# Where each engine reads the kind of the next block: at the head of the loop, or inside the arms into a register that lives across iterations

## The chip, the cores and the metric

One core of a Trainium2 chip runs the kernel. The metric is the device time of one execution in microseconds (us); the median of three executions before the change is 526.78 us (526.13 to 526.92).

## What is computed

The reference is a sigmoid attention followed by a mixture of experts in which only some tokens take part. Attention has 8 batches, 12 heads, 448 positions and a head size of 64; its output, turned to 3584 tokens of 768 numbers, is the input x of the second part:

```python
scores = scale * np.matmul(q, k.transpose(0, 1, 3, 2)) - np.log(S)
attn = 1.0 / (1.0 + np.exp(-scores))
x = (attn @ v)                       # reshaped to 3584 x 768
...
do_compute = x @ w_skip > 0          # the other tokens keep x
e_idx = argmax(x @ w_gate)           # one of 8 experts
gate_w = softmax(x @ w_gate)[e_idx]
out = x + gate_w * (relu(x @ w1[e_idx]) @ w2[e_idx])
```

Here w1 is 768 x 1024 and w2 is 1024 x 768 for each expert, in float32.

## The kernel before

The first part, up to about 321 us of the span, is straight-line code: attention, the routing of the tokens to experts, and the first blocks of tokens. Behind it stands a loop (L1537) whose trip count and whose work depend on the data; here it runs 14 times, from about 321 to 523 us. One iteration handles one block of up to 128 tokens of one expert, and there are four kinds of block, each with its own code (an "arm"):

- FULL (`block(i, False)`): a block of 128 tokens, with the weights split into a high and a low part (wh, wl) so that three products make one in float32. First product L516, turn of h L530, second product L544.
- SPLIT (`block(i, True)`): the same, and the weights of the next expert are split in its course (L1231, L1234, L1237).
- HALF (`half`): up to 64 tokens, both products at L1458, two at a time side by side in the array, turn of h at L1481.
- FEW (`few`): up to 32 tokens, both products at L1391, four at a time side by side, turn of h at L1412 (first half) and L1416 (second half).

The kinds in the order of this input are SPLIT, HALF, FULL, HALF, FULL, FEW, FULL, FEW, FULL, FEW, SPLIT, FEW, FULL, FEW.

A table `slots` of three rows (L1086) holds per block whether there is a next expert, which one, and the kind (row TYP). `entry` (L1088) reads one number of it into a register of each engine named, with an assertion on its bounds; on an engine this is a TENSOR_LOAD with a FUSED_REGOPS for the address ahead of it (both shown at L1089). At the head of the loop all five engines load the kind of block i, `slots[TYP, i + 2]`, and take two compare-and-branch instructions (`choose`, L1525 to L1533) into the arm. The five engines run through the loop each at its own pace; semaphores alone tie them together. Within an arm the order is written by hand (`tc.manual_schedule`). SP also reads in each FEW and HALF and in each SPLIT the next expert (`next_expert`) and starts the transfers of its weights (L1213, L1222).

The helpers that the steps below name: `turn_x` transposes the gathered tokens of the next block on PE (L492, into pxt); `fetch` lets POOL gather the tokens of the block after it (L564) and its records (L1115); `ready_x` and `whole_x` bring the turned tokens into the forms that the products want (ACT L498 and L1097, DVE L502); `shift` moves a list of indices on by one on DVE (L1283); `weigh_sum` multiplies the products py with the gate on DVE (L1325); `put` adds the block to the output by an indirect transfer of POOL (L574); `advance` moves the records on (L1315 to L1318).

```python
def entry(j, col, engines, most):
    return nc.values_load(slots[j : j + 1, col], engines=engines, min_val=0, max_val=most)
...
with tc.For_i(0, nreg, 1, iteration_sync="reg_based") as i:
    kind = entry(TYP, ds(i + 2, 1), mybir.ALL_ENGINES, SPLIT)
    choose(kind, i)
```

Of the kernel before, what the change touches and what calls it, by code (L numbers as in the profile page):

```python
# [23 lines left out]
def kernel(  # L24
# [11 lines left out]
    nc = tc.nc  # L36
# [471 lines left out]
    def gemm1(h, part, xh, xl, ph, lag=False):  # L508

        kinds = ((xh, wh1), (xh, wl1), (xl, wh1))  # L510
        t = [(2 * j + 3 * (n == 2) if lag else 2 * n * NK1, n, j) for n in range(3) for j in range(NK1)]
        t.sort()
        for n in part:
            _, kind, j = t[n]
            a, w = kinds[kind]
            nc.tensor.matmul(  # L516
                ph[h],
                a[:, j * P : (j + 1) * P],
                w[j][h],
                start=(n == 0),  # L520
                stop=(n == len(t) - 1),
            )

    def relu(h, hs, ph):
        nc.scalar.activation(hs[:, h * H1 : (h + 1) * H1], ph[h], AF.Relu)  # L525
# [579 lines left out]
    def ready_x():  # L1105
        for h in range(2):
            hi_x(h, pxt[h], xh)
        for h in range(2):
            whole_x(h, [slice(j, j + 1) for j in range(3)])
        for h in range(2):  # L1110
            lo_x(h, pxt[h], xh, xl)
# [128 lines left out]
        nc.vector.tensor_tensor(wl2[i], raw2[i], wh2[i], op=ALU.subtract)  # L1240

    dve, pool = nc.vector, nc.gpsimd

    order.__exit__(None, None, None)
    nx = (
# [81 lines left out]
    def block(i, last):  # L1327


        def split1(js, h):  # L1330
            if last:
                for j in js:
                    hi1(j, h)
                for j in js:
                    lo1(j, h)

        gemm1(0, range(G1), xh, xl, ph, last)
        relu(0, hs, ph)
        split1(range(3), 0)
        gemm1(1, range(9), xh, xl, ph, last)  # L1340
        turn_h(0, hs, pht[0])
        split_h(0, pht[0], hh, hl)
        take_rec()
        split1(range(3, NK1), 0)
        gemm1(1, range(9, G1), xh, xl, ph, last)
        relu(1, hs, ph)
        for h in range(2):
            turn_x(xn, h, pxt[h])
        fetch()
        split1(range(3), 1)  # L1350
        gemm2(0, hh, hl, py)
        turn_h(1, hs, pht[1])
        split_h(1, pht[1], hh, hl)
        split1(range(3, NK1), 1)
        if last:
            for h in range(2):
                whole_x(h, (slice(0, 3),))
            shift(dve)
        else:
            ready_x()  # L1360
        for j in range(1, NK2):
            gemm2(j, hh, hl, py)
        if last:
            for j in range(2):
                hi2(j)
            for h in range(2):
                hi_x(h, pxt[h], xh)
            for j in range(2, NK2):
                hi2(j)
            for j in range(4):  # L1370
                lo2(j)
            for h in range(2):
                lo_x(h, pxt[h], xh, xl)
        else:
            shift(dve)
        for o in range(2):
            rows = ys if last else yt
            weigh_sum(rows[:, o * H2 : (o + 1) * H2], half_y(py, o), recs[:, 0, 0:1])
        put(P, last)
        advance(1 if last else 2)  # L1380
        if last:
            for j in range(4, NK2):
                lo2(j)

    def few(i):

        nx = next_expert(ds(i + 2, 1))
        take_rec()

        def quarter(dst, g, n, a, w, j, most):  # L1390
            nc.tensor.matmul(  # L1391
                dst[g * SM : (g + 1) * SM, :n],
                a,
                w,
                start=(j == 0),
                stop=(j == most - 1),
                tile_position=(0, g * SM),
            )

        Q1 = FF // 4  # L1400
        turned = (pht[0], ph[0])
        parts = [slice(c * P, (c + 1) * P) for c in range(2)]
        for c, s in enumerate(parts):
            for j in range(NK1):
                for g in range(4):
                    at = (g % 2) * Q1 + c * P
                    quarter(ph[c], g, P, xf[:, j, :SM], raw1[j][g // 2][:, at : at + P], j, NK1)
            nc.scalar.activation(hs[:, s], ph[c][:, :P], AF.Relu)
        for h in range(2):
            for g in range(2):  # L1410
                load_w1(g, h, nx)
        nc.tensor.transpose(turned[0][:, :P], hs[:, parts[0]], ident)  # L1412
        for h in range(2):
            turn_x(xn, h, pxt[h])
        fetch()
        nc.tensor.transpose(turned[1][:, :P], hs[:, parts[1]], ident)  # L1416
        ht4 = ht[:, : 8 * SM].rearrange("p (c g t) -> p c g t", c=2, g=4)
        for s, p in zip(parts, turned):
            nc.scalar.activation(ht[:, s], p[:, :P], AF.Copy)
        ready_x()  # L1420
        shift(dve)

        for n, j in enumerate((0, 2, 1, 3)):
            for g in range(4):
                o, h = g // 2, g % 2
                m = j + h * (NK2 // 2)
                quarter(
                    py[h],
                    g,
                    H2,  # L1430
                    ht4[:, j % 2, 2 * h + j // 2, :],
                    raw2[m][:, o * H2 : (o + 1) * H2],
                    n,
                    NK2 // 2,
                )
        for g in range(4):
            load_w2(g, nx)
        for m in range(2):
            for o in range(2):
                g = 2 * o + m  # L1440
                s = slice(o * H2, (o + 1) * H2)
                p = py[m][g * SM : (g + 1) * SM, :H2]
                if not m:
                    nc.scalar.activation(yt[:SM, s], p, AF.Copy, scale=recs[:SM, 0, 0:1])  # L1444
                    continue
                nc.vector.scalar_tensor_tensor(
                    yt[:SM, s], p, recs[:SM, 0, 0:1], yt[:SM, s], op0=ALU.mult, op1=ALU.add
                )
        put(SM)
        advance()  # L1450

    def half(i):

        nx = next_expert(ds(i + 2, 1))
        take_rec()

        def side(dst, g, n, a, w, j, most):
            nc.tensor.matmul(  # L1458
                dst[g * MD : (g + 1) * MD, :n],
                a,  # L1460
                w,
                start=(j == 0),
                stop=(j == most - 1),
                tile_position=(0, g * MD),
            )

        for j in range(NK1):
            for h in range(2):
                side(ph[0], h, H1, xf[:, j, :], raw1[j][h], j, NK1)
        turned = (pht[0], ph[1])  # L1470
        parts = [slice(0, 2 * P), slice(2 * P, 4 * P)]
        for s in (slice(0, P), slice(P, 2 * P), parts[1]):
            nc.scalar.activation(hs[:, s], ph[0][:, s], AF.Relu)
        for h in range(2):
            for g in range(2):
                load_w1(g, h, nx)
        for h in range(2):
            turn_x(xn, h, pxt[h])
        fetch()
        for c in range(4):  # L1480
            nc.tensor.transpose(  # L1481
                turned[c // 2][:, (c % 2) * P : (c % 2 + 1) * P],
                hs[:, c * P : (c + 1) * P],
                ident,
            )
        for s, p in zip(parts, turned):
            nc.scalar.activation(ht[:, s], p[:, : 2 * P], AF.Copy)
        ready_x()
        shift(dve)

        ht8 = ht.rearrange("p (c h t) -> p c h t", c=4, h=2)
        for n in range(NK2):
            c, h = divmod(n, 2)
            m = h * (NK2 // 2) + c
            for o in range(2):
                side(
                    py[1],
                    o,
                    H2,
                    ht8[:, c, h, :],  # L1500
                    raw2[m][:, o * H2 : (o + 1) * H2],
                    n,
                    NK2,
                )
        for g in range(4):
            load_w2(g, nx)
        for o in range(2):
            s = slice(o * H2, (o + 1) * H2)
            weigh_sum(ys[:MD, s], py[1][o * MD : (o + 1) * MD, :H2], recs[:MD, 0, 0:1])
        put(MD)  # L1510
        advance()
# [13 lines left out]
    def choose(kind, i):  # L1525
# [5 lines left out]
        with c.Else():  # L1531
            with tc.If(kind < SPLIT) as d:
                run(HALF, i)  # L1533
            with d.Else():
                run(SPLIT, i)

    with tc.For_i(0, nreg, 1, iteration_sync="reg_based") as i:  # L1537
        kind = entry(TYP, ds(i + 2, 1), mybir.ALL_ENGINES, SPLIT)
        choose(kind, i)


# [26 lines left out]
```

## Time and profile before

| what | value |
|---|---|
| median of three executions | 526.78 us (526.13 to 526.92) |
| the profiled execution, its own time | 526.53 us |
| its span on the core | 524.8 us |
| granted TensorE clock, mean | 0.995 |
| instructions | 15310 |
| DMA traffic | 107.21 MB, mean 204 GB/s |

The profile is of one execution. In its rows PE is TensorE's matmuls, PEld its weight loads, DVE VectorE, ACT ScalarE, POOL GpSimd and SP SyncE; a "q" behind the engine's name is an instruction of the engine's sequencer (a register load, a branch, a semaphore), which doesn't count as busy. L12 is line 12 of the kernel. An entry "out<-in" names what an instruction writes and reads. The share of the clock and the busy shares of PE over the span, in 40 slices of 13.1 us:

```profile
PE   8999999999999999999989999999999999999991
PEclk9999999999999999999999999999999999999997
```

PE is busy in all slices but the last, and at full clock; the loop covers the last 16 of them.

### The profile page before, as it was taken

Reading aid. Unit: us, or ns where it says so; the run is one execution under the profiler, and the core shown is the slowest. Engines: PE = TensorE matmul, PEld = TensorE weight load, DVE = VectorE, ACT = ScalarE, POOL = GpSimd, SP = SyncE. Lnnn points to the kernel's source line nnn. Section 1 sums busy time; section 2 is a strip of 40 time slices with the busy share of each in tenths; the row PEclk is TensorE's granted clock in tenths of the full one; section 3 lists DMA queues with packets and bytes.
Section 4 is the critical chain, followed back from the end, with each engine's and each line's share of the span. In section 5 each row is a group of like instructions: output and inputs, shape, how many; then the busy total and the mean of one; then the engine's idle time right before and its main releaser. Section 6 shows DMA issues by size and latency. Waiting matters only on the chain.

```text
span 524.8 us, 15310 instructions
## 1 busy us (share of the span) xinstructions
PE 508.7 (97%) x5033; PEld 339.2 (65%) x5034; DVE 296.1 (56%) x721; ACT 281.0 (54%) x485; POOL 262.5 (50%) x414
## 2 busy tenths in 40 slices
PE   8999999999999999999989999999999999999991
PEld 7765555545545456555445989948669797978790
DVE  4556757648667676687684962862222322269422
ACT  5776776767767668677664211942112323268322
POOL 4523553443557666766574332553333645455644
PEclk9999999999999999999999999999999999999997
DMA  8999787898999999999955023979393959695942
GB/s 211 209 257 200 150 187 156 178 175 173 195 206 234 220 203 221 196 204 213 199 105 114 11 92 105 389 210 347 99 364 119 317 230 310 240 328 227 346 184 47
DMA packets 140288, 107.21 MB, mean 204 GB/s; under 512 B 97099, under 2 KB 112731, under 8 KB 140240
## 3 DMA queue, kind: packets, MB, share of 16 engines
q1 hardware_dynamic: 134000, 97.66, 70.0%
q0 software_dynamic: 4576, 8.65, 6.9%
q8 instruction: 30, 0.49, 0.4%
q10 hardware_dynamic: 1664, 0.26, 0.3%
q14 instruction: 18, 0.15, 0.1%
HBM read 98.49 MB, written 17.56 MB: 221 GB/s over the span
## 4 chain that ended last, share of the span: by engine, by line
PE 89%; DVE 3%; SPq 2%; DMA 2%; issue 1%; ACT 1%; POOL 0%; POOLq 0%; ACTq 0%; DVEq 0%
PE s L212 23%; PE pa L240 21%; PE ph L516 11%; PE py L544 11%; PE b_ph L516 3%; PE b_py L544 3%; PE ph L1391 3%; PE py L1458 2%; PE ph L1458 2%; PE pxt L492 2%; PE py L1391 2%; PE pl L280 1%; PE pht L530 1%; DMA out_dram<-y 1%; SPq L263 1%
## 5 line engine op out<-in xcount | busy, mean ns | idle before, releaser
L232 ACT ACTIVATE at<-s,bias 128x896 f32<-128x896 f32 (+1 forms) x191 | 173.3, 913 | 82.1 <-PE s L212 71.2
L212 PE MATMUL s<-x 64*64 64x448 f32 (+1 forms) x1528 | 165.4, 498 | 1.3 <-DVE wh L485 0.9
L240 PE MATMUL pa<-at,v 64*64 64x448 f32 (+1 forms) x1536 | 163.0, 489 | 0.0
L176 POOL COPY kq<-kq 32x896 f32<-32x896 f32 (+1 forms) x96 | 88.1, 917 | 94.6 <-DMA kq<-in_q_dram 59.0
L212 PEld LDWEIGHTS s<-x 64*64 64x64 f32 x1528 | 80.0, 191 | 53.1 <-issue 28.6
L240 PEld LDWEIGHTS pa<-at,v 64*64 64x64 f32 x1536 | 62.5, 133 | 54.9 <-issue 47.8
L194 DVE STREAM_TRANSPOSE x<-kq 128x448 f32<-128x448 f32 x94 | 80.8, 934 | 5.0 <-POOL kq L176 5.0
L250 DVE TENSOR_TENSOR xt<-xt,pa 128x448 f32<-128x448 f32 x48 | 29.7, 620 | 54.4 <-ACT xt L673 49.6
L414 POOL DMA_INDIRECT lst<-rec,idx x32 | 31.7, 989 | 17.4 <-DVE xt L250 5.8
L486 POOL TENSOR_TENSOR wl<-wr,wh 128x384 fp32r<-128x384 f32 (+1 forms) x28 | 31.2, 1125 | 12.6 <-DVE wh L485 8.1
L255 DVE STREAM_TRANSPOSE y<-xt 128x448 f32<-128x448 f32 x48 | 31.0, 645 | 6.8 <-DMA out_dram<-y 5.2
L574 POOL DMA_INDIRECT out_dram<-ys,rp x15 | 23.7, 1580 | 16.6 <-issue 8.4
L525 ACT ACTIVATE hs<-ph 128x512 f32<-128x512 f32 x14 | 8.3, 596 | 43.9 <-PE ph L516 37.5
L536 DVE TENSOR_TENSOR hl<-pht,hh 128x512 fp32r<-128x512 f32 x14 | 9.7, 690 | 36.5 <-ACT hh L535 22.8
L544 PE MATMUL py<-wh,hh 128*128 128x384 f32 x112 | 29.8, 347 | 0.0
L502 DVE TENSOR_TENSOR xl<-pxt,xh 128x384 fp32r<-128x384 f32 x30 | 15.3, 552 | 25.3 <-ACT xf L1097 17.8
L544 PE MATMUL py<-wh,hl 128*128 128x384 f32 x112 | 28.8, 338 | 0.0
L544 PE MATMUL py<-wl,hh 128*128 128x384 f32 x112 | 28.7, 337 | 0.0
L516 PE MATMUL ph<-wh,xh 128*128 128x512 f32 x84 | 25.7, 402 | 1.1 <-ACT yt L1444 0.8
L516 PE MATMUL ph<-wl,xh 128*128 128x512 f32 x84 | 26.6, 403 | 0.0
L673 ACT ACTIVATE xt<-pa 128x448 f32<-128x448 f32 x48 | 25.7, 536 | 0.8 <-PE pa L240 0.8
L516 PE MATMUL ph<-wh,xl 128*128 128x512 f32 x84 | 24.5, 395 | 0.0
(277 smaller groups left out, 686.4 us busy)
## 6 DMA issues: line engine op xcount, KB each, us to landing
raw<-in_moe_w_dram SPq DMA_DIRECT2D x64, 768.0 KB
v<-in_v_dram SPq DMA_DIRECT2D x48, 256.0 KB
out_dram<-y SPq DMA_DIRECT2D x192, 56.0 KB
kq<-in_k_dram SPq DMA_DIRECT2D x46, 224.0 KB
kq<-in_q_dram SPq DMA_DIRECT2D x46, 224.0 KB
wr<-in_moe_w_dram SPq DMA_DIRECT2D x12, 256.0 KB
wr<-in_moe_w_dram SPq DMA_DIRECT2D x16, 192.0 KB
lst<-fill SPq DMA_DIRECT2D x4, 464.0 KB
```

The source lines that it names most:

```text
L176: nc.gpsimd.tensor_copy(a[BT:, :, :, :BT], a[:BT, :, :, BT:])
L194: nc.vector.transpose(xs[:, n].rearrange("p (r j) -> p j r", j=NJ), t.rearrange("p (j d) -> p j d", d=D)[:, :, :BT],)
L212: nc.tensor.matmul(sc[m * D : (m + 1) * D, j, : qs.stop - qs.start], xs[r, 0, first::NR7], xs[r, 1, qs], start=True, stop=True,)
L232: nc.scalar.activation(at[:, :, :n], sc[:, :, :n], AF.Sigmoid, bias=bias, scale=SCALE)
L240: nc.tensor.matmul(pa[j * D : (j + 1) * D, r, qs], vt[rs, j, r + c if c < 3 else 3 * (1 - r), :], at[rs, j, : qs.stop - qs.start], start=( ...
L250: nc.vector.tensor_tensor(x, x, pa[:, 1, :S], op=ALU.add)
L255: nc.vector.transpose(y, xts[b][:, hp, :])
L414: put = nc.gpsimd.indirect_dma_start(out=lst[:, :], out_offset=bass.IndirectOffsetOnAxis(ap=idx[:, c : c + 1], axis=0), in_=rec[:, c, :], ...
L486: nc.gpsimd.tensor_tensor(lo, r, hi, op=ALU.subtract)
L516: nc.tensor.matmul(ph[h], a[:, j * P : (j + 1) * P], w[j][h], start=(n == 0), stop=(n == len(t) - 1),)
L544: last = nc.tensor.matmul(half_y(py, o), a[h][:, js], w[j][:, o * H2 : (o + 1) * H2], start=(j == 0 and n == 0), stop=(j == NK2 - 1 and n ...
L1391: nc.tensor.matmul(dst[g * SM : (g + 1) * SM, :n], a, w, start=(j == 0), stop=(j == most - 1), tile_position=(0, g * SM),)
```

## The change

Each engine gets one register, `kinds`, that holds the kind of the block to come. It is loaded once ahead of the loop, from column 2. In each arm a new call, `next_kind`, loads column i + 3 into it, for each engine at a place of its own; the head of the loop only takes the register for the two comparisons.

```diff
+    kinds = nc.alloc_registers("kind", engines=mybir.ALL_ENGINES)
+
+    def next_kind(i, *engines):
+        for e in engines:
+            nc.engines[e].reg_mov(kinds[e], entry(TYP, ds(i + 3, 1), [e], SPLIT))
...
     def block(i, last):
...
+        next_kind(i, ET.SP)
         gemm1(0, range(G1), xh, xl, ph, last)
...
         relu(1, hs, ph)
+        next_kind(i, ET.PE)
         for h in range(2):
             turn_x(xn, h, pxt[h])
         fetch()
+        next_kind(i, ET.Pool)
         split1(range(3), 1)
...
             shift(dve)
+            next_kind(i, ET.DVE)
         else:
             ready_x()
+        next_kind(i, ET.Activation)
         for j in range(1, NK2):
             gemm2(j, hh, hl, py)
...
         else:
             shift(dve)
+            next_kind(i, ET.DVE)
         for o in range(2):
...
     def few(i):
         nx = next_expert(ds(i + 2, 1))
+        next_kind(i, ET.SP)
         take_rec()
...
         fetch()
+        next_kind(i, ET.Pool)
+        next_kind(i, ET.PE)
         nc.tensor.transpose(turned[1][:, :P], hs[:, parts[1]], ident)
...
         ready_x()
         shift(dve)
+        next_kind(i, ET.Activation, ET.DVE)
...
     def half(i):
         nx = next_expert(ds(i + 2, 1))
+        next_kind(i, ET.SP)
         take_rec()
...
         fetch()
+        next_kind(i, ET.PE, ET.Pool)
         for c in range(4):
...
         ready_x()
         shift(dve)
+        next_kind(i, ET.Activation, ET.DVE)
...
+    nc.regs_mov(kinds, entry(TYP, slice(2, 3), mybir.ALL_ENGINES, SPLIT))
     with tc.For_i(0, nreg, 1, iteration_sync="reg_based") as i:
-        kind = entry(TYP, ds(i + 2, 1), mybir.ALL_ENGINES, SPLIT)
+        kind = nc.snap(kinds, min_val=0, max_val=SPLIT)
         choose(kind, i)
```

Lines of the changed kernel behind the new function stand 7 to 21 lines later than before (the loop is L1558, the second turn of h in FEW L1432).

Three places in the program's order show what moved. The first is DVE at the entry into the loop, behind the last instruction of the straight-line code (L559), with the semaphores that an instruction waits for; before:

```order
L502 TENSOR_TENSOR xl<-pxt,xh 128x384 [waits PE_49,Activation_49]
L502 TENSOR_TENSOR xl<-pxt,xh 128x384
L559 SCALAR_TENSOR_TENSOR ys<-b_py,rc_3732,x_3781 128x384 [waits DMASW5_49,PE_49]
L559 SCALAR_TENSOR_TENSOR ys<-b_py,rc_3732,x_3781 128x384
L1537 COMPARE_AND_BRANCH [waits DVE_I-4406_own,DVE_sequencer_I-4406_own]
L1537 UNCONDITIONAL_BRANCH
L1563 BRANCH_PREFETCH_HINT
L1089 ISA
L1089 TENSOR_LOAD slots [waits DVE_49]
```

and in the changed kernel:

```order
L502 TENSOR_TENSOR xl<-pxt,xh 128x384 [waits PE_49,Activation_49]
L502 TENSOR_TENSOR xl<-pxt,xh 128x384
L559 SCALAR_TENSOR_TENSOR ys<-b_py,rc_3732,x_3781 128x384 [waits DMASW5_49,PE_49]
L559 SCALAR_TENSOR_TENSOR ys<-b_py,rc_3732,x_3781 128x384
L1089 TENSOR_LOAD slots [waits DVE_49]
L1558 COMPARE_AND_BRANCH [waits DVE_I-4425_own,DVE_sequencer_I-4425_own]
L1558 UNCONDITIONAL_BRANCH
L1584 BRANCH_PREFETCH_HINT
```

The load now stands ahead of the first branch of the loop, and so ahead of the semaphores that go with it; the address computation (ISA) has gone, since the column is fixed. The other engines' entries change in the same way.

The second place is PE in FEW, from the turn of the first half of h (L1412) to the second product; before:

```order
L1391 MATMUL ph_4373<-raw_0_1_4348,xf 32x128 x2
L1391 MATMUL ph_4373<-raw_1_1_4366,xf 32x128 x2
L1412 ISA
L1412 MATMUL pht<-ident,hs 128x128
L492 REGISTER_ALU
L492 MATMUL pxt<-ident,xn 128x128 x6
L1416 REGISTER_ALU
L1416 MATMUL ph_4372<-ident,hs 128x128
L1391 ISA
L1391 MATMUL py_4374<-raw_0_4367,ht 32x384
```

and in the changed kernel, where these lines are L1426, L1432 and L1405:

```order
L1405 MATMUL ph_4373<-raw_0_1_4348,xf 32x128 x2
L1405 MATMUL ph_4373<-raw_1_1_4366,xf 32x128 x2
L1426 ISA
L1426 MATMUL pht<-ident,hs 128x128
L492 REGISTER_ALU
L492 MATMUL pxt<-ident,xn 128x128 x6
L1089 ISA
L1089 TENSOR_LOAD slots
L1089 ISA x2
L1248 ISA
L1432 MATMUL ph_4372<-ident,hs 128x128
L1405 ISA
```

Five instructions have come between the turn of x (L492) and the second turn of h: the address, the load, two for the assertion, and one at L1248 for the register.

The third place is PE in FULL and SPLIT, from the end of the first product (L516) to the second (L544); one piece of the difference, with + for what is new:

```order
 L516 MATMUL ph_4373<-wh_4_1_101,xl 128x512
 L516 MATMUL ph_4373<-wh_5_1_103,xl 128x512
+L1089 ISA
+L1089 TENSOR_LOAD slots
+L1089 ISA x2
 L492 MATMUL pxt<-ident,xn 128x128 x6
 L544 ISA
```

The load stands there ahead of the turn of x, with nothing else moved.

More of the change, by code (lines that the diff above doesn't have):

```diff
@@ L1242 @@
     dve, pool = nc.vector, nc.gpsimd
+    ET = mybir.EngineType
+    kinds = nc.alloc_registers("kind", engines=mybir.ALL_ENGINES)
+    def next_kind(i, *engines):
+        for e in engines:
+            nc.engines[e].reg_mov(kinds[e], entry(TYP, ds(i + 3, 1), [e], SPLIT))
     order.__exit__(None, None, None)
```

## Prediction

> **What bounds the kernel now.** I read the page first (busy time, then the chain that ended last), then the cost of the loads that the change moves, then the heads of the loop and the waits around them.
>
> ```profile
> span 524.8 us, 15310 instructions
> PE 508.7 (97%) x5033; PEld 339.2 (65%) x5034; DVE 296.1 (56%) x721; ACT 281.0 (54%) x485; POOL 262.5 (50%) x414
> PE 89%; DVE 3%; SPq 2%; DMA 2%; issue 1%; ACT 1%; POOL 0%; POOLq 0%; ACTq 0%; DVEq 0%
> ```
>
> TensorE is busy 97% of the span and carries 89% of the chain; nothing else is above 56%. So an edit is worth what it does to the matmul array's rare idle places, and to the tail behind the last matmul. What the change moves are sequencer instructions. The rows of their line in before (the "q" is the engine's sequencer; nanoseconds, least/median/most):
>
> ```profile
> L1089 PEldq TENSOR_LOAD <-slots x14: 302/310/1265, 321.9 to 505.0; - x14
> L1089 DVEq TENSOR_LOAD <-slots x14: 305/317/331, 324.9 to 509.7; - x14
> L1089 ACTq TENSOR_LOAD <-slots x14: 12/278/291, 321.5 to 502.6; - x14
> L1089 POOLq TENSOR_LOAD <-slots x14: 295/302/311, 326.6 to 510.8; - x14
> L1089 PEldq FUSED_REGOPS  x14: 51/51/56, 321.7 to 504.9; - x14
> L1089 SPq FUSED_REGOPS  x42: 46/152/342, 335.1 to 516.7; - x42
> L1089 SPq SEQ_ASSERT  x28: 5/18/23, 335.4 to 516.9; - x28
> ```
>
> A load takes about 0.3 us of its sequencer, but PE's longest took 1.27 us. Whether that reaches the array shows in the chain of waits across heads (start, length, what):
>
> ```profile
> 399.91 3.87 PE py L544 x22
> 403.78 2.77 PE ph L1391 x96
> ...
> 407.58 2.75 PE py L1391 x32
> 410.34 6.49 PE ph L516 x27
> ...
> 432.71 2.75 PE py L1391 x32
> 435.47 0.28 issue
> 435.75 4.43 PE ph L516 x18
> ```
>
> At 403.78 (FULL to FEW) and 410.34 (FEW to FULL) the array goes on without a break, though PE's sequencer loads and branches there: it had queued enough work. At 435.47 the array ran dry for 0.28 us. One other head shows this, in the timeline:
>
> ```profile
> 461.75 0.47 PE L516 MATMUL ph<-wh,xh 128*128 128x512 f32 x1 [0.80 <-ACT yt L1444]
> ```
>
> The releaser named there, ACT, comes from the last semaphore; PE's own loads around those two places, beside the other two heads behind a FEW, are
>
> ```profile
> L1089 PEldq TENSOR_LOAD <-slots x1: 459/459/459, 409.1 to 409.1; - x1
> L1089 PEldq TENSOR_LOAD <-slots x1: 972/972/972, 434.3 to 434.3; - x1
> L1089 PEldq TENSOR_LOAD <-slots x1: 1265/1265/1265, 459.7 to 459.7; - x1
> L1089 PEldq TENSOR_LOAD <-slots x1: 446/446/446, 487.1 to 487.1; - x1
> ```
>
> The two long ones, 434.3 + 0.97 = 435.3 and 459.7 + 1.27 = 461.0, end shortly before the array starts again. They are the only heads at which I find the load on the array's path.
>
> **The change, part by part.** *PE's head without its load.* Gain: 0.28 + 0.80 = **1.08 us** at most, 0 at the other heads. I take all of it: the long load ends last there. The low end is 0, if the stall belongs to the place and not to the load. Nothing behind these two places takes the gain back as long as the whole is not earlier than before, since the weights' transfers keep their times.
>
> *The first loads, now ahead of the loop.* On every engine the load (and a move into the register) stands now before the semaphore updates that open the loop. The timeline of the first iteration's start shows who waits for those:
>
> ```profile
> 323.55 0.40 PE L516 MATMUL ph<-wh,xh 128*128 128x512 f32 x1
> 323.75 1.14 DVE L559 SCALAR_TENSOR_TENSOR ys<-b_py,rc,x 128x384 f32<-128x384 f32 x2 [0.52 <-PE b_py L544]
> 323.84 0.19 PEld L516 LDWEIGHTS ph<-wl,xh 128*128 128x128 f32 x1 [0.27 <-DVEq L1537]
> ...
> L1537 DVEq EVENT_SEMAPHORE  x2: 21/21/21, 323.8 to 323.9; - x2
> ...
> L1537 DVEq MOVE  x1: 43/43/43, 324.7 to 324.7; - x1
> ...
> L1060 DVEq TENSOR_LOAD <-left_i x1: 556/556/556, 306.1 to 306.1; - x1
> ```
>
> The second matmul of the loop has waited 0.27 us for DVE's update, and DVE could issue that only when L559 had been let go by PE. Now a load and a move come between: 0.32 (median of L1089) + 0.04 + two gaps between instructions of about 0.07 (the end of one row to the start of the next at the head) = 0.50 us. With 0.56 us, the load from a fixed address at L1060, it would be 0.74. If DVE's sequencer were not held by L559, it would be 0. I take **+0.5 us**: the update's start, 323.8, follows L559's, 323.75, at once, so the sequencer was held. Nothing behind can absorb it, since the array is dense from there on. For PE itself the load only changes places ahead of a queue that is full (loaded at 321.9, needed at 323.55).
>
> *PE's load in FEW.* It now stands behind the turn of x (L492) and ahead of the second transpose of h (L1416). In the first FEW:
>
> ```profile
> 406.68 0.28 ACT L1408 ACTIVATE hs<-ph 128x128 f32<-128x128 f32 x1 [0.95 <-PE ph L1391]
> ...
> 407.20 0.14 PEld L1416 LDWEIGHTS ph<-ident,hs 128*128 128x128 f32 x1
> ...
> 407.51 0.20 PEld L1391 LDWEIGHTS py<-raw,ht 128*32 128x32 f32 x8 [0.17 <-issue]
> ...
> L1416 PEldq ALU_OP  x1: 32/32/32, 406.4 to 406.4; - x1
> ...
> L1416 PEldq ALU_OP  x1: 32/32/32, 484.0 to 484.0; - x1
> L1416 PEld LDWEIGHTS ph<-ident,hs x1: 137/137/137, 485.4 to 485.4; 128*128 128x128 f32 x1
> ...
> L1391 PEldq FUSED_REGOPS  x1: 37/37/37, 407.0 to 407.0; - x1
> ```
>
> The sequencer reaches L1416 at 406.4 and gets to the next instruction (L1391) only at 407.0, right after ACT's hs has ended at 406.96: it is held there for nearly 0.6 us. New work in that hold: address 0.05, load 0.31, the two steps of the bounds assertion 0.15 and 0.02 (SP's rows), the move 0.04, and five gaps of 0.07: 0.92 us. The 0.6 are free, **0.3 us** are not, and the next matmul (L1391, "issue" 0.17) is bound by the sequencer already, so they reach the array. The second and third FEW look alike; the fourth is held 1.4 - 0.8 = 0.6 us longer and hides all; the fifth is the last iteration, whose end is not set by PE. So 3 x 0.3 = **+0.9 us**. The ends: 0 where the hold or the queue covers all; and, with loads as long as 0.97 to 1.27 us, another 0.66 to 0.96 us (0.97 and 1.27 less 0.31) in each of three, 2.0 to 2.9 us in all. I take 0.31, because the array is then at transposes as wide as the matmuls under which the other ten loads stayed near it, and not at the 32-column ones under which all four slower loads fell.
>
> [...]
>
> *PE's load in FULL, SPLIT and HALF.* In the blocks it stands ahead of the turn of x, and the sequencer's next long wait is
>
> ```profile
> L544 PEldq EVENT_SEMAPHORE  x7: 960/1047/1427, 330.2 to 495.3; - x7
> ```
>
> The least of these seven waits, 0.96 us, covers the 0.92. In HALF the head's evidence holds: a load of this size costs a full queue nothing. **0**; with that cover gone it would be 0.92 us in each.
>
> *The other engines.* ACT, POOL and DVE each lose 0.3 us at the head and get about 0.9 us in the arm. POOL's stands behind the issue of its gathers and waits for DVE anyway (41.0 us below); ACT's stands in stretches where ACT waits for PE (37.5); SP trades the load at the head for one ahead of weights that stream over many microseconds.
>
> ```profile
> POOL jk L1293 <- DVE sv L1315: 41.0, 9, 5.6
> ACT hs L525 <- PE ph L516: 37.5, 8, 8.1
> DVE yt L1325 <- PE py L544: 17.7, 5, 3.6
> ```
>
> DVE's stands between the shift of the indices and the weighing of y, where in FULL it waits for PE (17.7). In FEW nothing waits on PE's side for yt; only in the last FEW is it near the end of the chain, where POOL's use of yt comes about 1 us behind it: 0 here, 0.3 at worst. **0** in all.
>
> Sum: -1.08 + 0.5 + 0.9 = **+0.3 us**. The profiled execution took 526.53 us, 1.73 more than its span, and lies 0.25 below the median of the runs, 526.78. The sum gives 526.85 from the one and 527.1 from the other; I say **526.9**.
>
> **The rivals.** *The added loads are hidden, the removed stalls are gone.* Then -1.08 alone: 525.5 on the profiled execution; with the start's 0.5 kept, 525.95. For it: 403.78 and 410.34, where the queue hid the same load. Against it: the hold at L1416 and the update at 323.8. [...]
>
> *The stalls belong to the place.* PE's 0.97 and 1.27 us would then be something else that lands on whatever stands there, and the idle 1.08 us stays: +0.5 + 0.9 = +1.4, 527.9. For it: two other loads at the same place took 0.45 only, so the length is not the load's own. Against it: none of the rows beside it is as long.
>
> *Slower: PE's load in FEW is long there, too.* The price is the 2.0 to 2.9 us above on top of +0.3: 528.8 to 529.7. It decides from a load of 0.31 us on, since everything beyond the hold goes to the array one for one. For it: all four loads above 0.4 us fell around FEW. Against it: those fell under the packed second product, this one falls behind the first.
>
> **How the numbers follow.** What a measurement of this kernel can tell from no change is about 0.2%, 1.05 us. Forecast 0.50; hidden loads 0.20; the stalls stay 0.17; long loads in FEW 0.13. Forecast, with 0.2 to 0.6 us of spread in each term, is "same" but for 0.05 on the slower side. Hidden loads lie at -0.6 to -1.1, at the bound: 0.12 faster, 0.08 same. Stalls that stay, at +1.4: 0.09 slower, 0.08 same. Long loads: slower, 0.13. That makes faster 0.12, same 0.61, slower 0.27. The range of 8 in 10 takes in the hidden loads and the stalls that stay, and leaves out most of the long ones: 525.4 to 528.5.
>
> **What the changed profile would show.** The second L516 matmul of the loop starting about 0.5 us later behind the one before it, released by DVE's update; PE's load in FEW near 0.31 us and L1416's successor 0.3 us later against ACT's hs; no idle of 0.28 or 0.80 us at the first matmul behind any FEW; in the seven blocks, waits at L544 shorter by some 0.9 us and no idle of the array. The forecast is wrong if a new idle place appears on PE at L492 or L544, if the long loads turn up at their new places, or if the stalls behind FEW stay with no load there.

## The result, and the profile after

| | before | changed |
|---|---|---|
| median of ten executions | 524.80 us (524.05 to 527.27) | 528.08 us (526.84 to 530.07) |
| ratio of the times | | 1.0054 (95%: 1.0034 to 1.0073) |
| the profiled execution, its time and span | 526.53, 524.8 us | 528.34, 525.8 us |

The change makes the kernel slower by about 2.8 us (1.8 to 3.8). The ten runs of before contain the three that the prediction had; six of the other seven were faster (524.05 to 524.84 us), so the execution whose profile the prediction read, at 526.53 us, was one of the slower ones.

The page of the changed kernel has the same bound, 243 instructions more, and PE just as busy:

```profile
span 525.8 us, 15553 instructions
PE 509.2 (97%) x5033; PEld 333.3 (63%) x5034; DVE 296.9 (56%) x721; ACT 281.9 (54%) x485; POOL 262.5 (50%) x414
```

PE's loads of the kind are all short in this trace (most 0.36 us, where before had 1.27).

```profile
L1089 PEldq TENSOR_LOAD <-slots x15: 298/312/357, 319.7 to 509.1; - x15
```

The start of the loop in the timeline of PE: the second L516 matmul stands 0.79 us behind the first, where before had 0.29 (323.84 - 323.55), and waits for the update of DVE:

```profile
322.79 0.40 PE L516 MATMUL ph<-wh,xh 128*128 128x512 f32 x1
323.58 0.50 PE L516 MATMUL ph<-wl,xh 128*128 128x512 f32 x1 [0.39 <-DVEq L1558]
```

The first FEW in the same view, from the second turn of h (L1432) to the next block (L516), and the head behind the third FEW, where before had waited 0.80 us:

```profile
407.10 0.27 PE L1432 MATMUL ph<-ident,hs 128*128 128x128 f32 x1
407.43 3.00 PE L1405 MATMUL py<-raw,ht 128*32 128x384 f32 x32
410.36 0.50 PE L516 MATMUL ph<-wh,xh 128*128 128x512 f32 x1
...
461.30 0.50 PE L516 MATMUL ph<-wh,xh 128*128 128x512 f32 x1
```

From L1432 to the block it takes 3.26 us; no idle is marked at 461.30. So far this is what the steps of the prediction said. What they did not have is at the end of the program. There all engines meet twice, each with a DRAIN and semaphores of the kernel's last line. The rows of that line on ACT (x, least/median/most ns, first and last start), in before and then in the change, and the instruction transfers on queue q14 in the same order:

```profile
L1563 ACTq EVENT_SEMAPHORE  x3: 17/17/17, 523.2 to 524.8; - x3
L1563 ACTq DRAIN  x2: 8/11/14, 523.3 to 524.3; - x2
...
L1584 ACTq EVENT_SEMAPHORE  x3: 17/17/17, 522.3 to 525.7; - x3
L1584 ACTq DRAIN  x2: 8/75/142, 524.9 to 525.3; - x2
...
q14 instruction: 18, 0.15, 0.1%
q14 instruction: 20, 0.16, 0.1%
```

On ACT's way from the loop's exit to the program's end lie 2.5 us of nothing, between the semaphore at 522.3 and the DRAIN at 524.9. In before the same two stand 0.1 us apart (523.17 and 523.26). In the trace of the change two transfers of 8 KB of instructions start at 523.3 and 525.5 us; in before the last one on q14 starts at 333.6. The other engines wait for ACT there: DVE's and PE's DRAIN stand at 522.5 us, their next semaphore only at 525.2, behind ACT's.

### The profile page after: what moved, and what is told of

Its sections match the earlier page's. It is cut to its first block, busy times and chain, and to the rows that moved or that the text cites. A ratio compares the mean times of both kernels' runs of the same rounds, so it can differ in the third digit from the quotient of the medians.

```text
span 525.8 us, 15553 instructions
## 1 busy us (share of the span) xinstructions
PE 509.2 (97%) x5033; PEld 333.3 (63%) x5034; DVE 296.9 (56%) x721; ACT 281.9 (54%) x485; POOL 262.5 (50%) x414
## 5 line engine op out<-in xcount | busy, mean ns | idle before, releaser
L212 PE MATMUL s<-x 64*64 64x448 f32 (+1 forms) x1528 | 162.7, 497 | 1.2 <-DVE sel L407 0.9
L240 PE MATMUL pa<-at,v 64*64 64x448 f32 (+1 forms) x1536 | 160.4, 489 | 0.0
L212 PEld LDWEIGHTS s<-x 64*64 64x64 f32 x1528 | 76.5, 191 | 55.8 <-issue 31.8
L240 PEld LDWEIGHTS pa<-at,v 64*64 64x64 f32 x1536 | 58.3, 133 | 58.3 <-issue 52.1
L486 POOL TENSOR_TENSOR wl<-wr,wh 128x384 fp32r<-128x384 f32 (+1 forms) x28 | 31.2, 1126 | 14.1 <-DVE wh L485 8.4
L544 PE MATMUL py<-wh,hh 128*128 128x384 f32 x112 | 29.9, 348 | 0.0
L544 PE MATMUL py<-wh,hl 128*128 128x384 f32 x112 | 28.8, 338 | 0.0
L544 PE MATMUL py<-wl,hh 128*128 128x384 f32 x112 | 28.7, 337 | 0.0
L516 PE MATMUL ph<-wl,xh 128*128 128x512 f32 x84 | 26.6, 403 | 0.4 <-DVEq L1558 0.4
L673 ACT ACTIVATE xt<-pa 128x448 f32<-128x448 f32 x48 | 25.7, 536 | 0.8 <-PE pa L240 0.8
L516 PE MATMUL ph<-wh,xh 128*128 128x512 f32 x84 | 25.7, 402 | 0.0
L516 PE MATMUL ph<-wh,xl 128*128 128x512 f32 x84 | 24.5, 395 | 0.0
```

The costliest lines, as they stand in the source:

```text
L212: nc.tensor.matmul(sc[m * D : (m + 1) * D, j, : qs.stop - qs.start], xs[r, 0, first::NR7], xs[r, 1, qs], start=True, stop=True,)
L240: nc.tensor.matmul(pa[j * D : (j + 1) * D, r, qs], vt[rs, j, r + c if c < 3 else 3 * (1 - r), :], at[rs, j, : qs.stop - qs.start], start=( ...
L486: nc.gpsimd.tensor_tensor(lo, r, hi, op=ALU.subtract)
L516: nc.tensor.matmul(ph[h], a[:, j * P : (j + 1) * P], w[j][h], start=(n == 0), stop=(n == len(t) - 1),)
L544: last = nc.tensor.matmul(half_y(py, o), a[h][:, js], w[j][:, o * H2 : (o + 1) * H2], start=(j == 0 and n == 0), stop=(j == NK2 - 1 and n ...
L673: nc.scalar.activation(xts[b][:, hp, :], pa[:, 0, :S], AF.Copy)
```

## The experiments

To compare traces I cut the time into four: **A**, from the loop's first matmul to the last matmul of the first product in the third FEW; **B**, from there to the first matmul of the block behind the fourth FEW; **C**, from there to the end of the span; **D**, what the execution's time has beyond the span. All are differences of starts or ends in the trace, of one profiled execution each, in us:

| kernel | A | B | C | D |
|---|---|---|---|---|
| before (first trace) | 133.33 | 31.75 | 36.2 | 1.73 |
| e1, before again | 133.12 | 31.07 | 36.1 | 1.76 |
| e4, before and 20 copies on ACT | 132.78 | 30.84 | 38.0 | 1.76 |
| the change | 134.17 | 30.84 | 38.0 | 2.54 |
| e2, the change again | 134.09 | 31.34 | 38.0 | 1.76 |
| e9, the change, third chip | 134.40 | 31.21 | 38.1 | 1.70 |
| e3, ACT without assertion | 134.10 | 31.19 | 36.2 | 4.06 |
| e5 and e10, three copies on ACT | 133.66 and 134.18 | 31.04 and 33.26 | 36.1 and 36.2 | 2.27 and 1.74 |
| e6, DVE's first load early | 133.67 | 33.47 | 37.9 | 1.99 |
| e7, PE's load in FEW early | 133.64 | 33.34 | 38.0 | 1.91 |
| e11, all three | 132.62 | 33.80 | 36.1 | 1.66 |
| e8 and e12, PE alone | 133.06 and 133.00 | 31.77 and 31.75 | 36.1 | 1.98 and 1.72 |

e1 to e4 ran on one chip, e5 to e8 on a second, e9 to e12 on a third. Ratios are to before on the same chip. On the second and third, before itself spreads over 4 and 5 us (525.35 to 529.22, 526.05 to 531.07), and ratios have intervals of 0.2 to 0.5%; there the traces carry more than the times.

**e1: before, once more.** No edit.

> The kernel before, once more, for a second trace of it. Theory A (PE's loads of 0.97 and 1.27 us at the heads behind the second and third FEW, the idle of 0.28 and 0.80 us behind them and the late hs of ACT in the fourth FEW are chance of one execution): this trace has no PE load over 0.5 us at these heads and no idle at the first L516 behind them; the loop is 1 to 1.6 us shorter than in the first trace. Rival B (they belong to the place): the same two heads show loads of about 1 us and idle of 0.3 and 0.8 us again. Ratio to itself 1.000 within 0.002.

Measured: ratio 1.0005 (0.9987 to 1.0022). The head behind the third FEW, here in e1 and then in e4, whose loop is that of before too:

```profile
459.86 0.47 PE L516 MATMUL ph<-wh,xh 128*128 128x512 f32 x1 [0.45 <-issue]
...
459.44 0.47 PE L516 MATMUL ph<-wh,xh 128*128 128x512 f32 x1 [0.21 <-issue]
```

PE's loads at the heads behind the second and third FEW took 0.97 and 1.27 us in the first trace, 0.90 and 1.09 in e1, 0.31 and 0.81 in e4. So A and B are both half right: the long load belongs to the place (third FEW: three times out of three), and its length is chance. Behind the second FEW idle is marked in the first trace alone. What taking the load away can give at these places is 0.2 to 0.8 us behind the third FEW and nothing sure behind the second, not 1.08.

**e2: the change, once more.** No edit.

> The change, once more. Theory A: slower than before by 2.5 to 3.3 us, the sum of 0.5 (DVE's first load), 0.9 (PE's load in FEW) and 1.8 (ACT's stall of 2.5 us between its last semaphore and its last DRAIN, at the end of the program, beside two transfers of 8 KB of instructions), with that stall at the same place. Rival B: the stall at the end is gone, as chance of one execution, and the time is 1.0 to 1.5 us over before.

Measured: 1.0059 (1.0045 to 1.0073), + 3.1 us; A, B and C as in the first trace within 0.5 us, ACT's stall at the same place. It is no chance.

**e3: ACT's loads in the arms without the bounds assertion.**

```diff
-            nc.engines[e].reg_mov(kinds[e], entry(TYP, ds(i + 3, 1), [e], SPLIT))
+            if e == ET.Activation:
+                got = nc.values_load(
+                slots[TYP : TYP + 1, ds(i + 3, 1)],
+                engines=[e],
+                min_val=0,
+                max_val=SPLIT,
+                skip_runtime_bounds_check_because="the planner writes kinds 0 to 3",
+            )
+            else:
+                got = entry(TYP, ds(i + 3, 1), [e], SPLIT)
+            nc.engines[e].reg_mov(kinds[e], got)
```

> The change with ACT's loads in the arms without the bounds assertion: ACT's program is 8 instructions shorter, nothing else differs. Theory A (ACT fetches a new piece of its program at the very end, because its code has grown over the edge of a piece): the fetch and the stall at the end are gone, 1.7 to 1.9 us less than the change, 0.8 to 1.5 us over before. Rival B (the end stall has another cause): the same time as the change within 0.4 us.

Measured: 1.0069 (1.0056 to 1.0082), + 3.6 us, so in time theory A missed: e3 is not faster than the change (e2, 1.0059), and the two intervals overlap. In the trace the stall inside the span has gone, as A said:

```profile
L1594 ACTq EVENT_SEMAPHORE  x3: 17/17/17, 522.9 to 524.4; - x3
L1594 ACTq DRAIN  x2: 8/11/14, 522.9 to 524.0; - x2
```

C is back at 36.2. But D is 4.06 us in the profiled execution and 3.96 to 4.12 in all six, where the medians of the other kernels are 1.7 to 2.1 (single executions up to 3.4), and the trace shows the two 8 KB transfers at 526.2 and 528.3, behind the end of the span (524.5). With the 8 instructions less the transfers have only moved behind the span, and the execution has 2.3 us more there (4.06 against 1.76 in e1 and e2). That code which runs behind the kernel's last instruction is fetched there is my reading; the traces show nothing of what runs there.

**e4: before, with ACT's program as long as in the change.**

```diff
+    pad = const.tile([P, 20], F32, name="pad")
+    for k in range(20):
+        nc.scalar.activation(pad[0:1, k : k + 1], zf[0:1, 0:1], AF.Copy)
     with tc.For_i(0, nreg, 1, iteration_sync="reg_based") as i:
```

> The kernel before with 20 copies of one number on ACT ahead of the loop, which put the end of ACT's program at the same position as in the change (706 instructions ahead of it). They lie in a stretch where ACT is idle about half the time. Theory A: the stall at the end appears, before + 1.7 to 1.9 us, with a transfer of 8 KB of instructions in the last 3 us. Rival B: before + 0 to 0.4 us, no stall at the end.

Measured: 1.0047 (1.0034 to 1.0061), + 2.5 us (1.8 to 3.2), without any of the change's edits. The copies run at 5.3 to 7.3 us of the span, far ahead of the loop, and A is not longer for them. At the end is the same hole:

```profile
L1566 ACTq EVENT_SEMAPHORE  x3: 17/17/17, 520.5 to 524.0; - x3
L1566 ACTq DRAIN  x2: 8/74/141, 523.1 to 523.5; - x2
```

C is 38.0 as in the change, with two transfers of 8 KB at 521.4 and 524.0. Theory A holds, with a time at or above its 1.7 to 1.9. This is the largest part of the loss, and it is made by the length of ACT's code alone: 20 instructions more.

**e5 and e10: the change with three copies more at the start of ACT's program.** The edit is that of e4 with 3 for 20, on the change.

> The change, with three small copies more at the start of ACT's program, which push the instructions behind the loop's last branch over the edge that cost the change its stall. Theory A (the stall is ACT's fetch of the next piece of its program, and costs only because it comes last): ACT now fetches right after its last iteration, at about 513 us, while POOL still works; no stall near the end, 1.7 to 2.0 us less than the change although ACT's program is longer: before + 0.8 to 1.3 us. Rival B (more instructions on ACT cost more): the change + 0 to 0.3 us, before + 2.9 to 3.3.

> The change with three small copies at the start of ACT's program, on the chip of the reference. Theory A (ACT's late fetch costs about 1.8 us of the time): 1.4 to 2.2 us less than e9. Rival B (the fetch costs in the trace only; in the time something else comes last): less than 0.5 us apart.

Measured: e5 1.0045 (1.0021 to 1.0069), + 2.4 us, with an interval (1.1 to 3.6) that reaches into both theories' times; e10 1.0063 (1.0041 to 1.0084), beside e9, the change on the same chip, at 1.0069 (1.0044 to 1.0094).

> The change, as the reference for the other kernels of this call on the same chip. Both theories: before + 2.3 to 3.3 us, with ACT's stall near the end and the 0.5 us at the start of the loop.

In the trace the hole is closed, in a longer program; ACT's last lines of e5:

```profile
L1587 ACTq EVENT_SEMAPHORE  x3: 17/17/17, 524.3 to 525.9; - x3
L1587 ACTq DRAIN  x2: 8/11/14, 524.4 to 525.4; - x2
```

The one 8 KB transfer that takes its place starts at 325.1 us in e5, in the first iteration, where nobody waits for ACT. Theory A had it at about 513 us, behind the last iteration: the place was wrong, the closed hole right. C falls from 38.1 (e9) to 36.1 and 36.2. Of these 2 us the medians of e9 and e10 show 0.8, and the intervals overlap almost wholly: in time the two cannot be told apart there. e10's B is 2 us longer than e9's though the loop's code is the same, which takes the gain back in that execution; e11 below shows what B is.

**e6: DVE's first load and move behind the writing of slots.**

```diff
...
+    nc.vector.reg_mov(kinds[ET.DVE], nc.values_load(slots[TYP : TYP + 1, 2:3], engines=[ET.DVE]))
...
-    nc.regs_mov(kinds, entry(TYP, slice(2, 3), mybir.ALL_ENGINES, SPLIT))
+    for e in (ET.PE, ET.Activation, ET.Pool, ET.SP):
+        nc.engines[e].reg_mov(kinds[e], nc.values_load(slots[TYP : TYP + 1, 2:3], engines=[e]))
```

> The change, with DVE's first load (and its move) moved from behind L559 to behind the writing of slots, some 10 us earlier. Theory A: PE's second L516 matmul of the loop follows the first as in before; 0.4 to 0.6 us less than the change, before + 2.3 to 2.7. Rival B (DVE's sequencer was not held, or another engine's load is as late): no difference, the same 0.5 us between the first matmuls.

```profile
323.51 0.40 PE L516 MATMUL ph<-wh,xh 128*128 128x512 f32 x1
323.80 0.50 PE L516 MATMUL ph<-wl,xh 128*128 128x512 f32 x1
```

Measured: 1.0046 (1.0026 to 1.0066), + 2.4 us. The matmuls are 0.29 us apart again and A is 0.4 to 0.7 shorter than in the change (133.67 against 134.09 to 134.40). Theory A holds for this step. The time fits its + 2.3 to 2.7, but says little, since B is 33.5, for a reason that e11 shows.

**e7: PE's load in FEW at the start of the arm.**

```diff
     def few(i):
         nx = next_expert(ds(i + 2, 1))
-        next_kind(i, ET.SP)
+        next_kind(i, ET.SP, ET.PE)
...
-        next_kind(i, ET.PE)
         nc.tensor.transpose(turned[1][:, :P], hs[:, parts[1]], ident)
```

> The change, with PE's load in FEW moved to the start of the arm, where the old load at the head stood behind a full queue. Theory A: in each of the five FEW, the second product starts 0.13 us earlier and lasts 0.2 us less (0.20 and 2.34 us as in before); four of the five reach the end: 1.0 to 1.4 us less than the change, before + 1.5 to 2.0. Rival B (the array waits there for ACT's ht, not for the sequencer): no difference.

The first FEW in the timeline, from the second turn of h on:

```profile
408.63 0.27 PE L1431 MATMUL ph<-ident,hs 128*128 128x128 f32 x1
408.84 2.82 PE L1405 MATMUL py<-raw,ht 128*32 128x384 f32 x32
411.59 0.50 PE L516 MATMUL ph<-wh,xh 128*128 128x512 f32 x1
```

2.96 us to the block instead of 3.26, and so in each FEW: 0.3 us each is confirmed, and the same load at the start of the arm is free. A is 0.5 to 0.8 shorter than in the change (two FEW lie in A). The time, 1.0066 (1.0040 to 1.0092), + 3.5 us, missed the + 1.5 to 2.0 that was expected: B again, 33.3.

**e11: all three costs taken away** (e6, e7 and the three copies).

> The change with all three costs taken away: DVE's first load behind slots, PE's load in FEW at the arm's start, and the three copies on ACT. Theory A (these three are the whole loss): before - 1.0 to before + 0.2, with the first matmuls 0.29 us apart, second products of 0.20 + 2.34 us in FEW and no fetch near the end. Rival B (there is a fourth cost, such as the assertions or DVE's later work): before + 0.5 to 1.5.

Measured: 1.0029 (1.0010 to 1.0047), + 1.5 us. A (132.62), C and D are as good as in before or better; B is 33.8. So something beyond the three costs time, as rival B said, but not what it named: it is in the fourth FEW. This is the first FEW behind a SPLIT, and its first product waits there for ACT's splitting of the second weights (L1237; L1241 in e11), which waits for their transfer. The waits of PE in that FEW, first in the change, then in e12, then in e11:

```profile
482.08 1.74 PE L1405 MATMUL ph<-raw,xf 128*32 128x128 f32 x56 [0.30 <-ACT wh L1237]
...
482.51 0.43 PE L1409 MATMUL ph<-raw,xf 128*32 128x128 f32 x8 [1.41 <-ACT wh L1237]
483.24 1.77 PE L1409 MATMUL ph<-raw,xf 128*32 128x128 f32 x56 [0.31 <-issue]
...
483.62 3.65 PE L1406 MATMUL ph<-raw,xf 128*32 128x128 f32 x64 [1.06 <-ACT wh L1241]
```

The 6.29 MB of weights begin to move 6.5 to 7.8 us behind the third FEW's first matmul. Their last packet lands 24.6 to 25.7 us behind it in eight of the traces, and 26.4 to 27.5 us in the other six (e6, e7, e8, e10, e11, e12). In the eight, PE goes on behind the wait at 27.7 to 28.3 us, whatever the head in between did: the idle at the head and the idle in this FEW are 0.80 and 0.31 us in the first trace of before, 0.45 and 0.76 in e1, 0.21 and 0.80 in e4. In the six it goes on at 28.7 to 29.1 us and has waited 1.7 to 2.4. Why the weights land later there isn't shown. It need not be the edit: e5 and e10 are the same kernel and reach the FEW at the same 25.3 us, and their weights land at 25.4 and 26.5. ACT goes on 0.5 to 0.9 us behind the last packet wherever it waits. Its wait, in e5 and then in e10 (the releaser named is the last semaphore):

```profile
482.39 1.58 ACT L1237 ACTIVATE wh<-raw 128x768 fp32r<-128x768 f32 x2 [0.25 <-SPq L1552]
...
483.12 1.58 ACT L1237 ACTIVATE wh<-raw 128x768 fp32r<-128x768 f32 x2 [1.21 <-SPq L1552]
```

In e11 the matmuls behind the wait also take nearly twice as long (3.65 us for 64 of them, 1.77 for 56 in e12). The granted clock falls there to 0.50 for 3.41 us, and so it does in e6, e7 and e10; these four are just the traces with B over 33 us. In all four the fall comes 477.87 us, 140 times 3.4133 us, behind the start of the full clock, and every stretch of full or half clock that ends within a trace lasts a whole number of these steps (the full clock 512.00 us, 150 of them, in the first trace of before, and 508.59 us, 149, in that of the change). The stretches around the wait cut at the steps, for e12, then e10, then e11 (us; busy time and count of PE, PEld, DVE, ACT and POOL; granted clock; DMA share and GB/s):

```profile
479.23:482.64 3.41, 1.99 (x41) 1.26 (x42) 3.20 (x8) 2.20 (x4) 0.19 (x1) 1.00 0.25 94
482.64:486.06 3.42, 3.11 (x73) 2.49 (x69) 3.41 (x4) 1.19 (x4) 2.78 (x2) 1.00 0.25 17
...
482.02:485.43 3.41, 1.67 (x45) 1.11 (x43) 3.19 (x9) 1.58 (x2) 0.53 (x2) 1.00 0.01 3
485.43:488.84 3.41, 3.41 (x51) 3.03 (x41) 3.09 (x5) 0.83 (x3) 2.47 (x5) 0.50 0.29 17
...
479.99:483.40 3.41, 1.24 (x28) 0.49 (x18) 3.38 (x7) 2.34 (x4) 0.03 (x1) 1.00 0.18 70
483.40:486.82 3.42, 3.12 (x56) 2.73 (x60) 3.24 (x6) 1.09 (x3) 2.39 (x2) 0.50 0.00 0
```

In the step ahead of the fall PE is busy for 1.24 to 1.67 us of 3.41 in the four traces. In e8 and e12 PE idles in this FEW as long as in e10 (1.7 us), but a border between two steps lies in the wait, no step has less than 1.99 us of PE's work, and the clock holds. So the wait is set by the transfer; whether it costs another 1.5 to 2 us goes, in these six traces, with where it falls between the steps. The first step begins at 4.8 to 7.7 us of the span, from trace to trace (7.6 in e8 and 4.8 in e12, which are one kernel), so that is chance to the kernel. In the eight traces with 0.3 to 0.85 us of idle the clock held.

**e8 and e12: PE alone reads inside the arms.** In FEW at the arm's start, no assertion on any engine but for the expert's; the other engines load at the head as before.

```diff
...
-        kind = entry(TYP, ds(i + 2, 1), mybir.ALL_ENGINES, SPLIT)
+        for e in (ET.DVE, ET.Activation, ET.Pool, ET.SP):
+            nc.engines[e].reg_mov(kinds[e], kind_of(ds(i + 2, 1), e))
+        kind = nc.snap(kinds, min_val=0, max_val=SPLIT)
```

> Only PE reads the kind inside the arms, in FEW at the arm's start, and without the bounds assertion; the other engines load at the head as in before, without an assertion. Theory A (the gain of the change is PE's free heads behind FEW, 0.3 to 1.2 us, and all its costs lie in DVE's first load, PE's place in FEW and the length of ACT's program): before - 0.3 to - 1.2 us, no idle of PE at the first L516 behind a FEW. Rival B (the last edge: ACT's program is 2 instructions longer than in before, and its end might cross): before + 0.8 to + 1.8, with a fetch of 8 KB behind the span. Rival C (a load is as long at any place around FEW): before within 0.3 us, with idle before the matmuls elsewhere.

> PE alone reads inside the arms, once more. Theory A: before - 0.3 to - 1.0 us and within 0.4 of e11. Rival B (nothing is won at PE's heads, since the wait for weights in the fourth FEW takes it back): before within 0.3 us.

Measured: 0.9990 (0.9973 to 1.0006) and 0.9991 (0.9979 to 1.0002), - 0.5 us each with intervals that hold 1: no gain that can be shown. No idle is marked behind any FEW, A is 0.1 to 0.3 below that of the first two traces of before and above that of e4, and B, 31.8, is at the top of before's: at the fourth FEW PE waits 1.7 us, 0.9 more than in e4, for weights that land later. No 8 KB transfer comes near the end or behind it, so rival B of e8 did not happen. Between the rest the time doesn't decide: the two - 0.5 lie in theory A's range, their intervals take in "within 0.3 us" as well, and e12 is 2 us faster than e11, which theory A had within 0.4. Of all versions that read the kind inside the arms, this is the only one that isn't shown to be slower than before.

## Why the prediction went as it did

The likeliest case (no change, + 0.3 us) did not happen; the time fell on the slower side, to which the prediction had given 0.27. The given range, 525.4 to 528.5, holds 528.08, but by luck: before itself ran at 524.80 in these ten executions and not at the 526.78 that the forecast was added to. By the ratio the change costs 2.8 us, nine times the sum of the forecast. None of the signs of being wrong that it named came up (idle at L492 or L544, long loads, stalls behind FEW): all of them looked at PE in the loop. Step by step:

- *The first loads ahead of the loop, + 0.5.* Right in place and size: 0.79 - 0.29 = 0.50 us in the change, and gone in e6 by moving DVE's alone.
- *PE's load in FEW, + 0.3 each in three.* The size is right (3.26 against 2.96 us, e7), and so is the hold that it lies in. The step that failed is "the fourth is held 0.6 us longer and hides all": that longer hold was in one trace of before alone. In e1 and e4 L1416 follows L1412 by 0.82 us in the fourth FEW, as in the others, and by 1.22 in the first trace; in the change (0.82) the fourth pays as well. Where the hold was long in a later trace (1.46 us in e10, 1.47 in e6) the second product starts 0.20 us behind the turn, as without a load: the hiding is as forecast, the long hold is not the rule. The fifth is hidden, as forecast: C does not contain it (36.1 to 36.2 in e3, e5 and e10). The rival of long loads in FEW did not come: they took 0.30 to 0.32 us in the change's first trace.
- *PE's load in FULL, SPLIT and HALF, 0.* Right: a FULL takes 18.56 us in the change and 18.54 to 18.56 in the first trace of before, a HALF 12.23 to 12.24 in both. The cover was not the one named: the waits at L544 were to be 0.9 us shorter, and their median is 1.05 us in both. What shrank is the pause of PE's sequencer ahead of L544's address, from between 0.66 and 0.99 us (in one block 0.12) to between 0.07 and 0.12.
- *PE's head without its load, - 1.08.* The step was mis-sized. "I take all of it" took one execution's lengths for the place's. Over three traces of before, the idle is 0.28, 0 and 0 us behind the second FEW and 0.80, 0.45 and 0.21 behind the third. The rival that the stalls belong to the place and stay did not come: no trace of the changed kernel has idle there.
- *"Nothing behind these two places takes the gain back".* Wrong. The weights for the fourth FEW begin to move behind the third FEW's first product, ahead of the head that was to gain, and PE waits for them: in the three traces of before, the less idle at the third head, the more in the fourth FEW (0.80 and 0.31, 0.45 and 0.76, 0.21 and 0.80 us). From there to the block behind the fourth FEW, B is 31.8, 31.1 and 30.8 in before and 30.8, 31.3 and 31.2 in the change: neither the gain at the third head nor the loads in the third and fourth FEW are seen. What is left of the loop is A, + 1.1 us in the change (means of three traces each): 0.5 at the start, twice 0.3, and little of the gain.
- *"The other engines: 0 in all".* The step that failed most. Their time inside the loop was hidden, as said. Their length was not: with ACT's 20 instructions more, two transfers of 8 KB of instructions come at the end of its program (523.3 and 525.5 us), when everything else waits. C is + 1.9 us. No row of the trace of before shows this price; the prediction counted instructions by their run time only.

A + 1.1 and C + 1.9 make 3.0; measured were 2.8 and 3.1 (e2). That B is the same in both holds within its spread, 0.9 us in before's three traces and 0.5 in the change's.

Left open: why PE's load at the head behind a FEW takes up to 1.27 us (it was not tried alone), why the weights for the fourth FEW land 1 to 2 us later in six of the traces, and why the FULL iterations of the three kernels with three copies take 18.4 to 18.5 us and not 18.55. That the late fetch costs time is shown by adding it (e4); that taking it away saves time is shown in the traces' C alone, since e9 and e10 can't be told apart in time.

## What to carry to other kernels

Here 20 small copies on ACT cost 2.5 us (1.8 to 3.2) though they ran at 5.3 to 7.3 us of the span (e4): when an edit lengthens an engine's code, look at that engine's last instructions and at what the execution's time has beyond the span. In the change DVE and PE waited from 522.5 to 525.2 us, with ACT's DRAIN at 524.9. Before counting a removed stall as gain, look at it in a second trace, and find the next thing that is tied to a transfer which starts ahead of the stall. The load moved out of the loop's head was not free by that alone: behind the turn of x in FEW it cost 0.30 us, and at the start of the arm nothing (from the second turn of h to the next block 3.26 us in the change, 2.96 in e7 and in the first trace of before). Two heads of before, at 403.78 and 410.34 us, already were such places: the array had no idle there.

## What the runs showed of the hardware

- Code came to ACT in transfers of 8 KB on queue q14, whose count grew when ACT's code alone did (18 to 20 in e4). In the program with 706 ACT instructions ahead of the last two meetings of the engines (the change, e4) the fetch fell between the semaphore and the first DRAIN there, and cost 2.5 us of ACT and 1.9 us of the span. With 698 (e3) the two transfers fell behind the span, at 526.2 and 528.3 us, and the execution had 2.3 us more there; with 709 (e5, e10, e11) one was fetched in the first iteration (at 325.1 us in e5) and nothing was seen at the end; with 686 and 688 (before, e8, e12) none came near the end (the last on q14 at 333.6 us in before).
- The granted clock fell to 0.50 for 3.41 us in four traces (e6, e7, e10, e11), behind a step of 3.41 us in which PE was busy for 0.36 to 0.49 of the time; with 0.58 or more it held at this place. No fixed share follows from this: at the end of the kernel, in before, e7 and e8, steps with 0.42 to 0.49 passed without a fall. The same 1.7 us of idle came with a fall in e10 and with none in e12: of the steps around the wait, the one with the least of PE's work had 1.67 us of it in e10 and 1.99 in e12.
